# The last tile of a gated MLP: where its transposes stand in the queue, and in how many pieces its output is projected and stored

## The chip, the cores and the metric

The kernel runs on one core of a Trainium2 chip. A core has a matrix engine (PE in the profile; its weight loads are listed apart as PEld), VectorE (DVE), ScalarE (ACT), GpSimd (POOL) and SyncE (SP), each with its own queue of instructions that it works through in order. Engines wait for each other through semaphores. Transfers between the chip's DRAM and the on-chip memory are issued from a queue (here SP's or ScalarE's) and carried out by 16 DMA engines. [...]

The metric is the time of one execution on the device in microseconds, as the median over several runs; lower is better.

## The reference, cut to what matters

Two mixers follow each other on a sequence of 2048 rows with 640 columns, each behind a layer norm whose scale and shift come from a condition vector. The first is a long convolution by FFT; it ends before the part that the change touches. The second is a gated MLP with a mixing over the sequence:

```python
z = _gelu(jnp.einsum('bsd,df->bsf', x, w_in))
z1 = z[..., :Fh].copy()
z2 = _layernorm(z[..., Fh:], axis=-1)
g = jnp.einsum('ts,bsf->btf', w_sp, z2) + b_sp[None, :, None]
return jnp.einsum('bsf,fd->bsd', z1 * g, w_out)
```

with Fh = 864. The output is `x + gb * that`, in bf16. The change lies in the last two of these lines.

## The kernel before, in words

Everything up to `z1` and `z2` is ordered by a list written out by hand (`ORDER`) that a small planner walks through; the change does not touch it. When it is done, 16 tiles of `z1` and the normalised `z2` lie in on-chip memory, and so does `xt`, the residual.

The last stage, from about 195 us on, has no planner: its order is the order of the Python code. It goes over 16 tiles t of 128 rows of the output, and the functions `load_w`, `mix` and `project` each do a part for one tile.

`load_w(t)` fetches 128 rows of the mixing matrix by a transposing DMA on SP's queue, five tiles ahead.

`mix(t)` makes `g` for the tile in two halves of 432 columns (NFC = 2). Each half is 16 matmuls that accumulate over the sequence into one of four PSUM buffers (line 944). One VectorE instruction then adds the bias and multiplies with `z1`, and writes half of `u`, a bf16 tile of 128 x 896 (line 947; the last 32 columns are zeros from the start). Three buffers of `u` take turns. The next matmul needs `u` transposed. For tiles 0 to 14 a transposing DMA on SP's queue does it (line 950) and the function returns. For tile 15, `mix` has seven transposes on PE, 128 columns each, into a PSUM buffer `pt` (line 954), and a ScalarE copy from there to `uT` (line 955).

`project(t)` multiplies with the output weights, already scaled with `gb`. It has NH = 2 halves of HS = 320 columns. Each half is seven matmuls (line 962) into one of two PSUM buffers that take turns (tag `o`), and one VectorE addition of the residual into `ot` (line 964). One store of the 128 x 640 tile, 160 KB, follows on SP's queue (line 965).

The loop of lines 972 to 981 sets the order. In round t it emits `mix(t)`, then `load_w(t + 5)` while there is one, then `project(t - 2)`; two rounds more finish the projections. So behind the mixing of tile 15 PE's queue holds the seven transposes of tile 15 and then the projections of tiles 13, 14 and 15. A PSUM buffer is written again only when the instruction that read it has finished.

The end of the program (line 1007 in the profile) waits for all stores and then brings the engines together.

Of the kernel before, what the change touches and what calls it, by code (L numbers as in the profile page):

```python
# [10 lines left out]
ALU = mybir.AluOpType  # L11
# [112 lines left out]
def kernel(  # L124
# [20 lines left out]
    nc = tc.nc  # L145
    _, S, D = A_q.shape
# [3 lines left out]
    NT = S // P  # L150
    ND = D // P
    NFT = (Fh + P - 1) // P
    fsz = [min(P, Fh - i * P) for i in range(NFT)]
    SDIM = nc.vector.BN_STATS_DIM
    ADIM = nc.vector.BN_AGGR_DIM
    NH = 2
    HS = D // NH

    x_nat = A_q[0].rearrange("(n p) d -> p n d", p=P)
    out_nat = out[0].rearrange("(n p) d -> p n d", p=P)  # L160
# [12 lines left out]
    xt = persist.tile([P, NT, D], BF16)  # L173
# [31 lines left out]
    with ExitStack() as actx:  # L205
# [25 lines left out]
        op = plan.op  # L231
# [691 lines left out]
    UB = 3  # L923
# [5 lines left out]
    us = []  # L929
# [3 lines left out]
    wTs, uTs = {}, {}  # L933

    def load_w(t):
        wTs[t] = bwork.tile([P, NT, P], BF16, tag="wT", bufs=WB, name="wT")
        nc.sync.dma_start_transpose(wTs[t][:], B_w_sp[t * P:(t + 1) * P, :])

    def mix(t):
        u = us[t % UB]  # L940
        for fc in range(NFC):
            ps = psB.tile([P, 512], F32, tag="mm", bufs=4, name="ps")
            for s_ in range(NT):
                nc.tensor.matmul(ps[:, :FC], lhsT=wTs[t][:, s_, :], rhs=tl["z2_%d" % (s_ // TB)][:, s_ % TB, fc * FC:(fc + 1) * FC],  # L944
                                 start=(s_ == 0), stop=(s_ == NT - 1))
            sl = slice(fc * FC, (fc + 1) * FC)
            nc.vector.scalar_tensor_tensor(u[:, sl], ps[:, :FC], bcol[:, t:t + 1], z1[t][:, sl], op0=ALU.add, op1=ALU.mult)  # L947
        uTs[t] = bwork.tile([P, NFT, P], BF16, tag="uT", bufs=UB, name="uT")
        if t < NT - 1:
            nc.sync.dma_start_transpose(uTs[t][:], u[:])  # L950
            return
        pt = psB.tile([P, NFT, P], BF16, tag="pt", bufs=1, name="pt")
        for ft in range(NFT):
            nc.tensor.transpose(pt[:, ft, :], u[:, ft * P:(ft + 1) * P], ident[:])  # L954
        nc.scalar.copy(uTs[t][:], pt[:])  # L955

    def project(t):
        ot = bwork.tile([P, D], BF16, tag="ot", bufs=3, name="ot")
        for h in range(NH):
            ps = psB.tile([P, 512], F32, tag="o", bufs=2, name="po")  # L960
            for ft in range(NFT):
                nc.tensor.matmul(ps[:, :HS], lhsT=uTs[t][:fsz[ft], ft, :], rhs=w_o[:fsz[ft], ft, h * HS:(h + 1) * HS],  # L962
                                 start=(ft == 0), stop=(ft == NFT - 1))
            nc.vector.tensor_tensor(ot[:, h * HS:(h + 1) * HS], ps[:, :HS], xt[:, t, h * HS:(h + 1) * HS], op=ALU.add)  # L964
        nc.sync.dma_start(out_nat[:, t, :], ot[:])

    for t in range(WB - 1):
        load_w(t)
    w_o = wsp_pool.tile([P, NFT, D], BF16, name="w_o")
    for ft in range(NFT):  # L970
        nc.sync.dma_start(w_o[:fsz[ft], ft, :], B_w_out[ft * P:ft * P + fsz[ft], :])
    for t in range(NT + 2):
        if t < NT:
            mix(t)
        if t == 1:
            for ft in range(NFT):
                nc.vector.tensor_tensor(w_o[:fsz[ft], ft, :], w_o[:fsz[ft], ft, :], gb_bf[:fsz[ft], :], op=ALU.mult)
        if t + WB - 1 < NT:
            load_w(t + WB - 1)
        if t >= 2:  # L980
            project(t - 2)


# [28 lines left out]
```

## Time and profile before

| | |
|---|---|
| median of 6 runs | 326.12 us (325.81 to 326.99) |
| the profiled execution's own time | 326.19 us |
| its span, first to last instruction | 324.3 us |
| mean granted PE clock | 0.993 |
| PE busy, share of the span | 308.4 us, 95% |
| VectorE, ScalarE, GpSimd busy | 209.7, 148.2, 93.5 us |
| matmul of 128 x 432, line 944 | 346 ns, 512 of them |
| matmul of 128 x 320, line 962 | 299 ns, 224 of them |
| addition of 128 x 320, line 964 | 491 ns, 32 of them |
| store of 160 KB, from issue to landing | 1.8 to 3.0 us, median 2.2, 16 of them |

The durations of matmuls overlap, since they are pipelined: the time from the start of one to the start of the next is shorter than a row's duration. All times inside an execution are given in us from the start of the span. A wait is put down to the instruction whose semaphore came last.

### The profile page before, as it was taken

How to read it: one execution, taken by the hardware profiler on the slowest of the kernel's cores; microseconds unless marked ns; L12 is line 12 of the kernel's file. 1: busy time of each engine (PE TensorE's matmuls, PEld its weight loads, DVE VectorE, ACT ScalarE, POOL GpSimd, SP SyncE). 2: the span in 40 equal slices, each digit the busy share in tenths (PEclk: the TensorE clock that was granted, in tenths of full speed). 3: DMA queues.
4: the chain of work that ended last, by engine and by line, in shares of the span. 5: the costliest groups of instructions: out<-in, count | busy, mean ns of one | idle time of the engine just before them, and what ended most of it. 6: DMA issues, size and time to landing. Idle time of an engine off the chain costs nothing.

```text
span 324.3 us, 6365 instructions
## 1 busy us (share of the span) xinstructions
PE 308.4 (95%) x2574; PEld 205.5 (63%) x2582; DVE 209.7 (65%) x463; ACT 148.2 (46%) x255; POOL 93.5 (29%) x121
## 2 busy tenths in 40 slices
PE   5969999899999998899999999999999999999995
PEld 2556789778889896655555555555555555555553
DVE  8966999999999998899676773432222223333223
ACT  4756999897779755396578582000000000000010
POOL 2440725559799898310111120000000000000000
PEclk9989999999999999999999999999999999999999
DMA  6999997996687876004408970675654555522231
GB/s 114 207 258 264 258 276 196 241 249 172 116 232 151 260 143 226 4 3 79 82 1 147 197 202 2 122 142 107 155 115 115 113 115 114 113 51 49 49 51 61
DMA packets 128580, 44.99 MB, mean 139 GB/s; under 512 B 117704, under 2 KB 127784, under 8 KB 128552
## 3 DMA queue, kind: packets, MB, share of 16 engines
q1 hardware_dynamic: 125528, 41.78, 58.6%
q10 hardware_dynamic: 3024, 2.82, 2.6%
q8 instruction: 20, 0.33, 0.4%
q14 instruction: 8, 0.07, 0.1%
HBM read 16.11 MB, written 5.24 MB: 66 GB/s over the span
## 4 chain that ended last, share of the span: by engine, by line
PE 74%; DVE 12%; DMA 7%; SPq 4%; issue 1%; ACT 1%; POOL 0%; DVEq 0%; POOLq 0%
PE ps L944 29%; PE pu L240 15%; PE pz L240 13%; PE po L962 9%; DMA ZT<-Z 5%; PE sm L240 5%; SPq L511 3%; PE s L240 2%; DVE Tf L457 2%; DVE T L457 2%; DVE st L570 2%; DMA X<-in_A_ssm_k_dram 2%; DVE big L543 1%; DVE X L243 1%; PE sm L823 0%
## 5 line engine op out<-in xcount | busy, mean ns | idle before, releaser
L944 PE MATMUL ps<-X,wT 128*128 128x432 bf16 x512 | 95.7, 346 | 0.0
L944 PEld LDWEIGHTS <-wT 128*128 128x128 bf16 x512 | 50.1, 98 | 42.2
L955 ACT COPY uT<-pt 128x896 bf16<-128x896 bf16 x1 | 0.9, 906 | 118.0 <-PE pt L954 118.0
L240 PE MATMUL pu<-X,M 128*128 128x128 bf16 (+1 forms) x480 | 46.8, 239 | 1.5 <-DVE T L457 0.9
L240 PEld LDWEIGHTS <-Z 128*128 128x128 bf16 x320 | 31.1, 98 | 26.6 <-DVE Z L832 0.4
L240 PEld LDWEIGHTS <-M 128*128 128x128 bf16 x480 | 37.5, 99 | 7.0 <-issue 1.6
L947 DVE SCALAR_TENSOR_TENSOR u<-ps,bcol,G 128x432 bf16<-128x432 f32 x18 | 12.0, 668 | 42.2 <-PE ps L944 42.2
L243 ACT CAST X<-s 128x1024 bf16<-128x1024 f32 x32 | 32.7, 1021 | 4.4 <-PE s L240 4.3
L962 PE MATMUL po<-w_o,uT 128*128 128x320 bf16 (+1 forms) x224 | 32.8, 299 | 0.0
L240 PE MATMUL pu<-big,Z 128*128 128x432 bf16 x160 | 32.8, 346 | 0.0
L466 POOL TENSOR_TENSOR W<-Tf 128x256 bf16<-128x256 f32 x38 | 27.9, 754 | 16.5 <-DVE Tf L457 15.8
L240 PE MATMUL pz<-big,Z 128*128 128x432 bf16 x160 | 32.6, 346 | 0.0
L947 DVE SCALAR_TENSOR_TENSOR u<-ps,bcol,M 128x432 bf16<-128x432 f32 x14 | 9.3, 667 | 30.2 <-PE ps L944 30.2
L240 PEld LDWEIGHTS <-G 128*128 128x128 bf16 x360 | 26.9, 98 | 1.9
L962 PEld LDWEIGHTS <-uT 128*128 128x128 bf16 (+1 forms) x224 | 21.8, 98 | 9.8
L243 ACT CAST KH<-pu 128x512 bf16<-128x512 f32 x40 | 23.0, 595 | 6.4 <-PE pu L240 6.2
L457 DVE TENSOR_TENSOR Tf<-pu,KH 128x1024 f32<-128x1024 f32 x20 | 24.2, 1218 | 1.6 <-PE pu L240 1.1
L457 DVE TENSOR_TENSOR T<-pu,KH 128x1024 bf16<-128x1024 f32 x20 | 24.2, 1216 | 0.5 <-PE pu L240 0.5
L964 DVE TENSOR_TENSOR ot<-po,xt 128x320 bf16<-128x320 f32 x32 | 15.7, 491 | 13.5 <-PE po L962 13.5
L240 PEld LDWEIGHTS <-X 128*128 128x128 bf16 x288 | 18.3, 99 | 8.3 <-DVE X L396 4.8
L243 ACT CAST Z<-pz 128x512 bf16<-128x512 f32 x35 | 20.3, 590 | 6.8 <-PE pz L240 6.5
L888 DVE BATCH_NORM_STATS2 stz<-X 128x6 f32<-128x432 bf16 x32 | 18.2, 592 | 7.1 <-ACT X L882 7.1
(143 smaller groups left out, 412.3 us busy)
## 6 DMA issues: line engine op xcount, KB each, us to landing
wm<-in_w_mod_dram SPq DMA_DIRECT2D x4, 800.0 KB, 5.6
out_dram<-ot SPq DMA_DIRECT2D x16, 160.0 KB, 2.2
big<-in_B_w_in_dram SPq DMA_DIRECT2D x2, 1080.0 KB, 8.2
X<-in_A_ssm_k_dram SPq DMA_DIRECT2D x4, 512.0 KB, 6.3
kv_scr<-big SPq DMA_DIRECT2D x4, 512.0 KB, 3.1
X<-kv_scr SPq DMA_DIRECT2D x4, 512.0 KB, 4.6
xt<-in_A_q_dram SPq DMA_DIRECT2D x3, 640.0 KB, 6.7
wm<-in_w_mod_dram ACTq DMA_DIRECT2D x2, 800.0 KB, 7.4
```

Of the source, the lines that this page charges most:

```text
L240: nc.tensor.matmul(o, lhsT=w, rhs=x, start=start, stop=stop)
L243: (e.copy if e is nc.scalar else e.tensor_copy)(dst, src)
L457: e.tensor_tensor(T_[:], tl[pu][:, :, :, None, :].to_broadcast([P, KP, 2, 2, DU]), tl[KH][:, :, None, :, :].to_broadcast([P, KP, 2, 2, DU] ...
L466: e.tensor_tensor(tl[W][:, :, o, :], T_[:, :, 0, o, :], T_[:, :, 1, 1 - o, :], op=ALU.add if o else ALU.subtract)
L511: e.dma_start_transpose(tl[name][:, o + h * m:o + (h + 1) * m], src[0, h * m:(h + 1) * m, dt * P:(dt + 1) * P])
L543: e.tensor_tensor(vsl, tl[ps][:], vsl, op=ALU.mult)
L570: e.bn_stats(out=st[:, a, :], in_=xt[:, n, a * HS:(a + 1) * HS])
L888: op("D", "stz", lambda e, i=i, n=n, fc=fc: e.bn_stats(out=stz[:, n, fc, :], in_=tl[z2][:, i, fc * FC:(fc + 1) * FC]), r=[(z2, (i, fc))], ...
L944: nc.tensor.matmul(ps[:, :FC], lhsT=wTs[t][:, s_, :], rhs=tl["z2_%d" % (s_ // TB)][:, s_ % TB, fc * FC:(fc + 1) * FC], start=(s_ == 0), st ...
L947: nc.vector.scalar_tensor_tensor(u[:, sl], ps[:, :FC], bcol[:, t:t + 1], z1[t][:, sl], op0=ALU.add, op1=ALU.mult)
L962: nc.tensor.matmul(ps[:, :HS], lhsT=uTs[t][:fsz[ft], ft, :], rhs=w_o[:fsz[ft], ft, h * HS:(h + 1) * HS], start=(ft == 0), stop=(ft == NFT ...
L964: nc.vector.tensor_tensor(ot[:, h * HS:(h + 1) * HS], ps[:, :HS], xt[:, t, h * HS:(h + 1) * HS], op=ALU.add)
```

## The change

The transposes and the copy of tile 15 leave `mix` and become a function `turn_last`, which the loop calls in round 15 behind `project(13)`. In `project`, tile 15 has three pieces in place of two: 320, 160 and 160 columns, each with its own seven matmuls and its own addition. Each piece of tile 15 is stored by itself as soon as it is added: the first and the third from SP's queue, the second from ScalarE's. The other tiles are projected and stored as before, and the two PSUM buffers of tag `o` stay two.

```diff
         uTs[t] = bwork.tile([P, NFT, P], BF16, tag="uT", bufs=UB, name="uT")
         if t < NT - 1:
             nc.sync.dma_start_transpose(uTs[t][:], u[:])
-            return
+
+    def turn_last(t):
+        u = us[t % UB]
         pt = psB.tile([P, NFT, P], BF16, tag="pt", bufs=1, name="pt")
         for ft in range(NFT):
             nc.tensor.transpose(pt[:, ft, :], u[:, ft * P:(ft + 1) * P], ident[:])
...
     def project(t):
         ot = bwork.tile([P, D], BF16, tag="ot", bufs=3, name="ot")
-        for h in range(NH):
+        last = t == NT - 1
+        for i, (lo, hi) in enumerate(((0, HS), (HS, HS + HS // 2), (HS + HS // 2, D)) if last else ((0, HS), (HS, D))):
             ps = psB.tile([P, 512], F32, tag="o", bufs=2, name="po")
             for ft in range(NFT):
-                nc.tensor.matmul(ps[:, :HS], lhsT=uTs[t][:fsz[ft], ft, :], rhs=w_o[:fsz[ft], ft, h * HS:(h + 1) * HS],
+                nc.tensor.matmul(ps[:, :hi - lo], lhsT=uTs[t][:fsz[ft], ft, :], rhs=w_o[:fsz[ft], ft, lo:hi],
                                  start=(ft == 0), stop=(ft == NFT - 1))
-            nc.vector.tensor_tensor(ot[:, h * HS:(h + 1) * HS], ps[:, :HS], xt[:, t, h * HS:(h + 1) * HS], op=ALU.add)
-        nc.sync.dma_start(out_nat[:, t, :], ot[:])
+            nc.vector.tensor_tensor(ot[:, lo:hi], ps[:, :hi - lo], xt[:, t, lo:hi], op=ALU.add)
+            if last:
+                (nc.scalar if i == 1 else nc.sync).dma_start(out_nat[:, t, lo:hi], ot[:, lo:hi])
+        if not last:
+            nc.sync.dma_start(out_nat[:, t, :], ot[:])
...
         if t >= 2:
             project(t - 2)
+        if t == NT - 1:
+            turn_last(t)
```

## The prediction

> **What bounds the kernel now.** I read the whole-span table first: PE is busy 95% of the span, every other engine 65% or less. But the change touches only the last tile, so what counts is the chain of work that ended last, in order of time, for the last 20 us (start us, length us, what):
>
> ```profile
> 308.12 5.86 PE ps L944 x32
> 313.97 0.02 issue
> 314.00 0.68 DVE u L947
> 314.68 0.05 issue
> 314.72 0.40 PE pt L954 x4
> 315.12 5.74 PE po L962 x42
> 320.86 0.02 issue
> 320.88 0.49 DVE ot L964
> ```
>
> The mixing of tile 15 ends on PE, the chain leaves PE for 0.7 us of VectorE, returns to PE for four transposes and 42 projection matmuls (tiles 13, 14, 15; 14 each), and ends with one addition on VectorE. So PE is the bound here except in two places: the hop through VectorE, and everything behind 320.86. The timeline shows the hop (start, length, engine, line, operands; in brackets the idle time and its releaser):
>
> ```profile
> 313.61 0.34 PEld L954 LDWEIGHTS <-u 128*128 128x128 bf16 x3
> 313.79 0.33 PE L954 MATMUL pt<-ident,u 128*128 128x128 bf16 x3
> 314.00 0.67 DVE L947 SCALAR_TENSOR_TENSOR u<-ps,bcol,G 128x432 bf16<-128x432 f32 x1 [2.25 <-PE ps L944]
> 314.72 0.23 PEld L954 LDWEIGHTS <-u 128*128 128x128 bf16 x4 [0.77 <-DVE u L947]
> 314.72 0.40 PE L954 MATMUL pt<-ident,u 128*128 128x128 bf16 x4 [0.60 <-DVE u L947]
> 314.95 0.57 PE L962 MATMUL po<-w_o,uT 128*128 128x320 bf16 x3
> 315.15 0.91 ACT L955 COPY uT<-pt 128x896 bf16<-128x896 bf16 x1 [117.98 <-PE pt L954]
> ```
>
> Three transposes need only columns that the first multiply-add wrote; the fourth needs the second one, which ends at 314.67. PE waits, and tile 13's projection, whose operands are there since about 302 (the transpose by DMA was issued at 299.19 and such a one lands after 2.9), stands behind it in PE's queue. ScalarE does nothing here but the copy.
>
> The third view is the end: VectorE's last two additions and SP's last issue in the timeline, then SP's waits at the program's end (count, min/median/max ns, first and last start), then the DMA share and rate over 321.3 to 324.3 us in 40 slices of 0.075 us.
>
> ```profile
> 319.93 0.49 DVE L964 TENSOR_TENSOR ot<-po,xt 128x320 bf16<-128x320 f32 x1 [0.46 <-PE po L962]
> 320.88 0.49 DVE L964 TENSOR_TENSOR ot<-po,xt 128x320 bf16<-128x320 f32 x1 [0.46 <-PE po L962]
> ```
> ```profile
> 321.40 0.33 SPq L965 DMA_DIRECT2D out_dram<-ot  x1
> ```
> ```profile
> L1007 SPq EVENT_SEMAPHORE  x7: 17/28/1435, 321.8 to 324.2; - x7
> ```
> ```profile
> DMA  0000000000003999995100000000000000000000
> GB/s 0 0 0 0 0 0 0 0 0 0 0 0 119 341 341 375 375 375 205 52 0 0 0 0 0 0 0 0 0 0 0 0 0 0 0 0 0 0 0 0
> ```
>
> The last store (160 KB, 128 rows of 1280 B) is issued at 321.40; its data move from about 322.2 to 322.75; SP is released near 323.24 (321.8 + 1.435), 1.8 us after the issue; then 1.06 us of closing to 324.3. So 0.8 us pass ahead of the data, 0.5 us are data, 0.45 us follow.
>
> **Part 1: tile 13's projection moves ahead of the transposes.** PE's queue becomes mixing 15, projection 13, seven transposes, projection 14, projection 15. Spacing of 320-column matmuls: 5.74/42 = 0.137 us, so 14 take 1.91. Transposes without a wait: four weight loads in 0.23 us, so 0.057 each, seven 0.40. Today from the first transpose to the first projection matmul: 314.95 - 313.79 = 1.16. Gain: 1.16 - 0.40 = 0.76 us.
>
> Its cover: projection 13 now stands over the 0.93 us until the multiply-add's end with 1.91. Without it the 0.76 is back. The moved step is seven transposes and one ScalarE copy; it issues no DMA and nothing is queued behind it on ScalarE but the new store. Projection 13 brings forward two additions and one store on SP by 1.16 us: the first addition would start near 314.95, just behind the multiply-add that ends at 314.67, and SP's queue has been empty since 309. What is late next: the transposed tile 15 is needed at projection 15, and only projection 14 is left to hide the copy. New times: projection 13 from 313.79, transposes from 315.70, projection 14 from 316.10 to 318.02; the last transpose ends near 316.27, the copy (0.91) near 317.21; the weights of projection 15 load from about 317.9. Slack 0.65 us, cost nothing.
>
> **Part 2: three pieces for tile 15.** Piece 0 is unchanged (7 x 0.137 = 0.96; starts 318.02, last matmul starts 318.84 and with its row's 0.30 ends 319.14; addition 319.16 to 319.65). Pieces 1 and 2 have 160 columns, a shape that the trace lacks. Between 128 columns (0.057 spacing, 219 ns long) and 320 (0.137, 299 ns) lies 0.070 spacing and 232 ns; seven take 0.49. Bounds: 0.057, as the transposes, and 0.098, one weight load's whole row; I take 0.070, since the transposes ran at 0.057 with the same weight loads. The addition of 160: the row for 320 is 491 ns, that for 512 from PSUM (multiply with v) 679, slope 0.98 ns a column, so 0.33 us (bounds 0.25, half of 491, and 0.49).
>
> The change adds one wait. There are two PSUM buffers for the pieces, so piece 2 needs the one of piece 0, free when its addition is done: 319.65, plus the 0.05 that the chain shows from VectorE to PE: 319.69. Unhindered it would start at 318.97 + 0.49 = 319.46. The stall is 0.23 us; nothing but piece 2 stands behind it on PE. Its last matmul starts 320.11, ends 320.34; addition 320.37 to 320.70. Today that end is 321.37; so of the 0.76, 0.67 arrive here: splitting costs 0.09 on the compute side (0.23 stall, less 0.16 shorter addition, rest rounding and matmul ends).
>
> **Part 3: the stores.** One of 160 KB becomes 80 KB (SP, rows of 640 B, issued about 319.68), 40 KB (ScalarE's queue, 320 B, about 320.03) and 40 KB (SP, 320 B, about 320.73). An issue takes 0.33 us on SP and 0.345 on ScalarE (row of kv_scr), both idle by then; data start 0.8 us after an issue, so the three data phases do not overlap (320.5, 320.8, 321.5). Only the last one sets the end. Today each of 16 DMA engines has 8 rows of 1280 B at 375/16 = 23.4 B/ns: 55 ns a row, 0.44 us. For 320 B rows the nearest row is the load of kv_scr, 256 B rows: at its plateau of 285 GB/s, 14.4 ns each, over its whole 2.4 us and 128 rows an engine 19 ns. Eight make 0.12 to 0.15 us. Gain 0.3 us (between 0.42, and a loss bounded below).
>
> [...]
>
> **Sum.** 0.76 - 0.09 + 0.30 = 0.97 us. The span goes from 324.3 to 323.3 and the profiled execution's 326.19 (1.9 around the span, unchanged) to 325.22. That execution stands 0.07 over the median of 326.12, so the median becomes 325.15, 0.30% lower. About 0.2% (0.65 us) is what a measurement of this kernel can tell from no change.
>
> **Rivals.**
> A. The sum above: 325.15; own range 324.8 to 325.4. Chance 0.62.
> B. The store is all latency: a 40 KB store also lands 1.8 us after its issue. For: 1.25 of its 1.8 us are not data, and stores of one size range from 1.8 to 3.0. Against: the data phase is plainly 0.5 us. Gain 0.67, 325.45, on the edge of what can be told. Chance 0.20.
> C. The other side: the 320 B rows of the last store are written slowly, row after row. [...] Against: packets of 256 B flow at 14 to 19 ns on the read side. Chance 0.08.
> D. Part 1 acts, but piece 2 waits for piece 1's addition too, if the buffer's release is counted to VectorE's newest instruction: start 320.04, end of the last addition 321.05, gain 0.32 + 0.30 = 0.62, 325.5. Against: today projection 14 starts at 316.87 while tile 13's second addition, begun at 317.06, is still to come, so releases are counted singly. Chance 0.10.
>
> **How the numbers follow.** Repeated runs before spread from 325.81 to 326.99, so a median may be off by 0.2 to 0.3. A falls below -0.2% nine times in ten (0.56), B and D half the time (0.10 and 0.05), C never: faster 0.71. Within 0.2%: what is left of A, B and D, 0.06 + 0.10 + 0.05 = 0.21. Slower: C, 0.08. Range: below, the full 0.76, a free split and 0.42 of store, 1.2, with a drift of 0.3, is 324.6; above, B or D with a drift is 325.85; C is left out.
>
> **What would show it.** Part 1: no idle PE before the transposes, 42 projection matmuls and seven transposes without a gap, the copy's end ahead of projection 15. Part 2: idle PE of about 0.2 us before piece 2, released by the first addition; the last addition near 0.33 us, ending 0.67 earlier against the span's start. Part 3: SP's long wait at the end down from 1.435 to 1.1, and ScalarE's store not the last to land; it would be only if it took over 2.1 us. The prediction is wrong if that wait grows, if PE still idles ahead of the transposes, or if the stages ahead of 308 us shift by more than 0.3 us.

## The result, and the profile after

The changed kernel takes 325.87 us (median of 35 runs) where the kernel before took 326.43 (72 runs): the ratio is 0.9977, with a 95% interval from 0.9966 to 0.9987, so 0.42 to 1.1 us of gain. The ratio is taken over the fast runs (one of the changed kernel, at 329.11 us, was slow), so it is not the quotient of the two medians. The forecast, 325.15 for 326.12 or 0.9970, lies inside the interval.

The profiled execution has a span of 322.8 us instead of 324.3. That is 1.5 us, but not all of it is the change's doing. The chain of waits of the changed kernel, in order of time (start us, length us, what):

```profile
307.65 5.84 PE ps L944 x32
313.50 1.91 PE po L965 x14
315.40 0.39 PE pt L956 x7
315.80 2.88 PE po L965 x21
318.68 0.02 issue
318.70 0.50 DVE ot L967
319.20 0.04 issue
319.24 0.66 PE po L965 x7
319.90 0.02 issue
319.93 0.33 DVE ot L967
```

The hop through VectorE's multiply-add has left the chain, and PE goes from the mixing into projection 13 (line numbers behind 950 have moved: 965 is the projection, 967 its addition, 956 the transposes, 957 the copy, 969 the stores in pieces). A new hop has come in near the end: the addition of 318.70, then the third piece's matmuls at 319.24. The timeline of the same stretch:

```profile
313.33 2.07 PE L965 MATMUL po<-w_o,uT 128*128 128x320 bf16 x14
313.54 0.67 DVE L947 SCALAR_TENSOR_TENSOR u<-ps,bcol,G 128x432 bf16<-128x432 f32 x1 [2.25 <-PE ps L944]
315.24 0.55 PE L956 MATMUL pt<-ident,u 128*128 128x128 bf16 x7
315.83 0.91 ACT L957 COPY uT<-pt 128x896 bf16<-128x896 bf16 x1 [119.12 <-PE pt L956]
318.70 0.81 DVE L967 TENSOR_TENSOR ot<-po,xt 128x320 bf16<-128x320 f32 x2 [0.46 <-PE po L965]
319.24 0.44 PEld L965 LDWEIGHTS <-uT 128*128 128x128 bf16 x6 [0.23 <-issue]
319.54 0.36 ACTq L969 DMA_DIRECT2D out_dram<-ot  x1
319.93 0.33 DVE L967 TENSOR_TENSOR ot<-po,xt 128x160 bf16<-128x160 f32 x1 [0.42 <-PE po L965]
```

The transposes run as one group without idle time; the copy ends at 316.74, well ahead of projection 15, which follows the 14 matmuls of projection 14 near 317.5. Ahead of the third piece's weight loads stand 0.23 us of idle time. The row calls it "issue", that is, it names no releaser; the chain does, as it goes back from the matmuls to the addition.

To keep the last tile apart from all that lies before, two stretches are compared. C runs from the start of tile 15's second multiply-add to the end of the last addition, T from there to the end of the span. A span of 324.3 us is rounded to a tenth, too coarse for T; a stretch that is left open at its end shows where the span ends to a hundredth (before, then after; stretch, length, busy time and number of instructions of the five engines, granted clock, DMA share, GB/s):

```profile
319.00:324.28 5.28, 1.85 (x14) 1.08 (x12) 1.45 (x3) 0.00 (x0) 0.00 (x0) 0.87 0.18 62
```
```profile
319.00:322.82 3.82, 0.80 (x10) 0.46 (x7) 0.84 (x3) 0.00 (x0) 0.00 (x0) 0.87 0.28 86
```

Before: C = 320.88 + 0.49 - 314.00 = 7.37 and T = 324.28 - 321.37 = 2.91. After: C = 319.93 + 0.33 - 313.54 = 6.72 and T = 322.82 - 320.26 = 2.56. So 0.65 + 0.35 = 1.00 us come from the change. The other 0.46 us (314.00 against 313.54) had been gained before the multiply-add even began. C and T are sums of rounded rows and good to about 0.02 us; the expectations of the runs below were written with T from the rounded spans, 2.93 before and 2.54 after.

The tail, in SP's waits of the changed kernel from 300 us on (us in total, times, longest):

```profile
SPq L1015 <- DMA out_dram<-ot: 1.1, 2, 0.6
SPq L1015 <- PEq L1015: 0.6, 2, 0.4
```

Before, the first of these was 1.5 in one piece. There are two pieces now, as SP waits for ScalarE's store first. The last store lands 1.5 us after its issue instead of 1.8. Its data, in the DMA view from 320.2 to 322.6 us in slices of 0.06 us, for an issue at 320.29:

```profile
GB/s 352 214 96 43 144 251 193 70 5 0 0 0 0 0 0 107 208 240 107 22 0 0 0 0 0 0 0 0 0 0 0 0 0 0 0 0 0 0 0 0
```

The first group is the 80 KB store's end and ScalarE's store; the second group is the last store, from about 321.1, 0.8 us after the issue, to 321.4. How long one DMA engine is busy with the last store is told by the queue's share in a stretch that holds this store alone: 3.0 us from 321.3 before, 0.45 us from 321.0 after (packets, MB, share of 16 engines):

```profile
q1 hardware_dynamic: 144, 0.16, 15.6%
```
```profile
q1 hardware_dynamic: 144, 0.04, 37.1%
```

That is 0.47 us an engine before and 0.17 after, for eight rows and one small packet each.

### The profile page after: what moved, and what is told of

Same layout as the page of the kernel before. It is cut to its first block, busy times and chain, and to the rows that moved or that the text cites. A ratio compares the mean times of both kernels' runs of the same rounds, so it can differ in the third digit from the quotient of the medians.

```text
span 322.8 us, 6384 instructions
## 1 busy us (share of the span) xinstructions
PE 307.8 (95%) x2581; PEld 205.8 (64%) x2589; DVE 209.8 (65%) x464; ACT 148.2 (46%) x255; POOL 93.6 (29%) x121
## 4 chain that ended last, share of the span: by engine, by line
PE 74%; DVE 10%; DMA 7%; SPq 4%; ACT 2%; issue 1%; POOL 0%; DVEq 0%; POOLq 0%; ACTq 0%
PE ps L944 29%; PE pu L240 15%; PE pz L240 13%; PE po L965 9%; DMA ZT<-Z 5%; PE sm L240 5%; SPq L511 3%; PE s L240 2%; DVE T L457 2%; DVE Tf L457 2%; DMA X<-in_A_ssm_k_dram 2%; DVE st L570 1%; DVE big L543 1%; DVE X L243 1%; ACT X L243 1%
## 5 line engine op out<-in xcount | busy, mean ns | idle before, releaser
L965 PE MATMUL po<-w_o,uT 128*128 128x320 bf16 (+2 forms) x231 | 33.2, 295 | 0.1
L967 DVE TENSOR_TENSOR ot<-po,xt 128x320 bf16<-128x320 f32 (+1 forms) x33 | 15.9, 482 | 12.7 <-PE po L965 12.7
```

The source lines that it names most:

```text
L965: nc.tensor.matmul(ps[:, :hi - lo], lhsT=uTs[t][:fsz[ft], ft, :], rhs=w_o[:fsz[ft], ft, lo:hi], start=(ft == 0), stop=(ft == NFT - 1))
L967: nc.vector.tensor_tensor(ot[:, lo:hi], ps[:, :hi - lo], xt[:, t, lo:hi], op=ALU.add)
```

## The experiments

In all of them the code up to tile 15's mixing is the same. C and T are taken from each trace as above, one execution of each kernel. Four pairs of kernels have the same matmuls, copy and additions over all of C, and agree in it to 0.01 us: 6.72 and 6.71, 6.61 twice, 6.47 twice and 6.49 twice.

**The order alone.**

```diff
     def project(t):
         ot = bwork.tile([P, D], BF16, tag="ot", bufs=3, name="ot")
-        last = t == NT - 1
+        last = False
```

> The transposes stand behind projection 13, tile 15 is projected and stored as before. Two stretches are read: C, from the start of tile 15's second multiply-add to the end of the last addition (before 7.37 us, after 6.72), and T, from there to the end of the span (before 2.93, after 2.54). Theory (terms add up): C = 7.37 - 0.76 = 6.61, T = 2.93, so 0.76 us less than before, ratio near 0.9977. Rival 1 (the gain is the smaller last store; the wait only moves to the copy ahead of projection 15): C near 7.3, ratio within 0.1% of 1. Rival 2 (the changed kernel's 1.5 us shorter span is the change's doing, also ahead of the last tile): the multiply-add of tile 15 starts near 313.5 again, not near 314.0.

Measured: ratio 0.9979, interval 0.9962 to 0.9997. The chain ends so:

```profile
315.54 1.91 PE po L965 x14
317.44 0.39 PE pt L956 x7
317.84 3.83 PE po L965 x28
321.67 0.02 issue
321.69 0.49 DVE ot L967
```

The multiply-add starts at 315.57, the last addition ends at 322.18, the span ends at 325.11: C = 6.61, T = 2.93. The order brings 0.76 us in C, which is what was worked out, and nothing in T. Rival 1 falls, and so does rival 2: this kernel's span is longer than that of the kernel before although its last tile is shorter by 0.74, since its multiply-add came 1.6 us later. What moves the multiply-add is not the change (see the last section).

**The pieces alone.** The transposes go back to where they stood.

```diff
         if t < NT - 1:
             nc.sync.dma_start_transpose(uTs[t][:], u[:])
+        else:
+            turn_last(t)
...
             project(t - 2)
-        if t == NT - 1:
-            turn_last(t)
```

> Three pieces and three stores for tile 15, but the transposes stay ahead of projection 13. Theory (terms add up): C = 7.37 + 0.04 to 0.09 (a stall of 0.23 us ahead of the third piece, a shorter last addition), T = 2.54, so 0.30 to 0.35 us less than before, ratio near 0.9990. Rival 1 (the smaller store is the main gain): 0.9977 or less. Rival 3 (splitting costs as much as the smaller store saves): ratio 1.000, T near 2.9.

Measured: ratio 0.9991, interval 0.9975 to 1.0007. From the trace (multiply-add at 315.14, last addition from 322.30 to 322.63, end of the span 325.18): C = 7.49, T = 2.55, a net 0.24 us less than before, where 0.30 to 0.35 were expected. The interval alone couldn't tell this from no change; the trace shows both terms: splitting costs 0.12 in C, over the 0.04 to 0.09 expected, and the smaller last store saves 0.36 in T. Rival 3 had T near 2.9 and falls; rival 1 asked for three times the trace's sum. The two parts add up: 0.74 for the order and 0.24 for the pieces are 0.98 of the 1.00 of the whole change. That the pieces gain anything rests on the traces; in the timed runs the order alone (0.9979) and the whole change (0.9977) can't be told apart.

**Three pieces, one store.**

```diff
-            if last:
-                (nc.scalar if i == 1 else nc.sync).dma_start(out_nat[:, t, lo:hi], ot[:, lo:hi])
-        if not last:
-            nc.sync.dma_start(out_nat[:, t, :], ot[:])
+        nc.sync.dma_start(out_nat[:, t, :], ot[:])
```

> The changed kernel, three pieces, but one store of 160 KB behind the third addition. Theory (the last store's bytes set T): C = 6.72 as in the changed kernel, T = 2.93 as before. Rival (T is shorter for another reason, as the order of the queues at the end): T = 2.54.

Measured, one execution: multiply-add at 313.75, last addition from 320.14 to 320.46, end of the span 323.38; C = 6.71, T = 2.92. T is back at the value of before, so it follows the last store and not the pieces or their order. Pieces without stores of their own only cost: 0.10 in C against the order alone.

**Two pieces, two stores.**

```diff
-        for i, (lo, hi) in enumerate(((0, HS), (HS, HS + HS // 2), (HS + HS // 2, D)) if last else ((0, HS), (HS, D))):
+        for i, (lo, hi) in enumerate(((0, HS), (HS, D)) if last else ((0, HS), (HS, D))):
```

> Transposes behind projection 13, tile 15 in two pieces of 320 columns, each stored at once: the first by SP, the second (80 KB, rows of 640 B) from ScalarE's queue. Theory (the store's data phase shrinks with its bytes): C = 6.61, T between 2.54 and 2.93, near 2.7. Rival (what shortens T is the third piece's short rows or that SP's queue was drained earlier): T = 2.9. Rival (ScalarE's queue lands later): T above 2.93.

Measured: ratio 0.9970, interval 0.9957 to 0.9983; C = 6.61 (314.11 to 320.72), T = 2.76 (end of the span 323.48), the store of 80 KB landing 1.6 us after its issue. T lies between, as the bytes do. Its sum of 9.37 us is 0.09 over that of the three pieces (9.28); the timed runs, whose intervals overlap widely, cannot rank the two.

**The cover of the copy taken away.** The transposes stand behind projection 14.

```diff
-        if t == NT - 1:
-            turn_last(t)
+        if t == NT:
+            turn_last(t - 1)
```

> The changed kernel with the transposes of tile 15 behind projection 14, so that nothing hides the ScalarE copy. Theory (projection 14 is the cover of the copy): PE idle of about 1.1 us ahead of projection 15, released by the copy, C = 6.72 + 1.1 = 7.8, T = 2.54. Rival (the copy is hidden or overlaps piece by piece): C below 7.0.

Measured, one execution. The timeline:

```profile
318.14 0.56 PE L956 MATMUL pt<-ident,u 128*128 128x128 bf16 x7
318.73 0.91 ACT L957 COPY uT<-pt 128x896 bf16<-128x896 bf16 x1 [121.03 <-DMA out_dram<-ot]
319.69 2.35 PE L965 MATMUL po<-w_o,uT 128*128 128x320 bf16 x21 [1.00 <-ACT uT L957]
```

PE is idle for 1.00 us, released by the copy; C = 7.90 (314.52 to 322.42), T = 2.56 (end of the span 324.98), and the last tile takes 10.46, more than the 10.28 of before. (The bracket at the copy names a store that landed at the same moment. The copy needs nothing of it, and starts 0.03 us behind the end of the transposes, as it does in the changed kernel, 0.04.) So the place between projections 13 and 14 is the only one of the three tried that hides both the multiply-add and the copy.

**A third PSUM buffer.** PSUM is where the matmuls' results stand until the addition reads them (`ot<-po` in the rows above).

```diff
-            ps = psB.tile([P, 512], F32, tag="o", bufs=2, name="po")
+            ps = psB.tile([P, 512], F32, tag="o", bufs=3, name="po")
```

> The changed kernel with three PSUM buffers for the projection's pieces in place of two. Theory (the third piece waits for the first one's addition through its buffer): idle PE ahead of the third piece gone, C = 6.72 - 0.22 = 6.50, T = 2.54. Rival (VectorE's additions in a row set the end, the buffer doesn't): C stays at 6.7, since the second piece's addition cannot start sooner.

Measured: ratio 0.9963, interval 0.9949 to 0.9978. The end of the chain:

```profile
315.39 0.39 PE pt L956 x7
315.78 3.85 PE po L965 x35
319.63 0.03 issue
319.66 0.33 DVE ot L967
```

All 35 matmuls follow each other; C = 6.47 (313.52 to 319.99), T = 2.56 (end of the span 322.55). The wait of 0.23 us was the buffer's: C falls by 0.25. It also gives the spacing of the 160-column matmuls: the 21 of 320 columns take 2.88 in the changed kernel's chain, so the 14 narrow ones take 0.97, 0.069 us each.

**A thin last piece.** Pieces of 320, 256 and 64 columns, with three buffers.

```diff
-        for i, (lo, hi) in enumerate(((0, HS), (HS, HS + HS // 2), (HS + HS // 2, D)) if last else ((0, HS), (HS, D))):
-            ps = psB.tile([P, 512], F32, tag="o", bufs=2, name="po")
+        for i, (lo, hi) in enumerate(((0, HS), (HS, 576), (576, D)) if last else ((0, HS), (HS, D))):
+            ps = psB.tile([P, 512], F32, tag="o", bufs=3, name="po")
```

> The changed kernel with three PSUM buffers and pieces of 320, 256 and 64 columns, so that the last store has 16 KB in rows of 128 B. Theory (data phase by bytes and rows that flow at 14 to 19 ns): the last addition waits for the one of 256 columns, C = 6.5 + 0.13 = 6.63, T = 2.45. [...]

Measured, one execution: C = 6.49 (315.40 to 321.89), T = 2.77 (end of the span 324.66). T is above the 2.45 of the theory, and a store of 16 KB, the smallest tried, lands later than one of 40: 1.7 us after its issue, where the changed kernel's last one took 1.5. The rows of 128 B might be slow to write by themselves; this run does not show whether they are. But the issues also show the middle store next to it: ScalarE's 64 KB were issued at 321.79, SP's 16 KB at 321.91, 0.12 us later, so that the two may be in each other's way. One more run separates the two reasons.

**The thin piece without its neighbour.** The middle piece's store is left out.

```diff
-            if last:
-                (nc.scalar if i == 1 else nc.sync).dma_start(out_nat[:, t, lo:hi], ot[:, lo:hi])
+            if last and i != 1:
+                nc.sync.dma_start(out_nat[:, t, lo:hi], ot[:, lo:hi])
```

> Pieces of 320, 256 and 64 columns with three PSUM buffers as in the run with a thin last piece, but the middle piece is not stored at all (its output is left out). Theory (the thin last store was late because the middle one, issued 0.12 us earlier, was moving its data): T = 2.45 and a landing 1.4 us after the issue. Rival (rows of 128 B are slow to write by themselves): T stays at 2.8, the landing at 1.7.

Measured, one execution: C = 6.49 (315.60 to 322.09), T = 2.56 (end of the span 324.65). The DMA issues from 317 us on, this kernel's and then those of the thin piece with its neighbour (KB each, us to landing):

```profile
out_dram<-ot SPq DMA_DIRECT2D x1, 80.0 KB, 1.6
out_dram<-ot SPq DMA_DIRECT2D x1, 16.0 KB, 1.4
```
```profile
out_dram<-ot SPq DMA_DIRECT2D x1, 80.0 KB, 1.6
out_dram<-ot ACTq DMA_DIRECT2D x1, 64.0 KB, 1.7
out_dram<-ot SPq DMA_DIRECT2D x1, 16.0 KB, 1.7
```

T is 0.21 under the run with the middle store, so the lateness was the neighbour's. What of the neighbour it was, its data or what follows them, this run doesn't tell. The 128 B rows alone land after 1.4 us, the soonest of all stores here: at eight rows an engine these short rows show no delay of their own. But T misses the expected 2.45 by 0.11: it is no shorter than with 40 KB, 2.56 in the changed kernel, so a last store smaller than 40 KB gained nothing.

**All stores from SP**, with three buffers.

```diff
-                (nc.scalar if i == 1 else nc.sync).dma_start(out_nat[:, t, lo:hi], ot[:, lo:hi])
+                nc.sync.dma_start(out_nat[:, t, lo:hi], ot[:, lo:hi])
```

> Three PSUM buffers and three pieces, all three stores from SP's queue. Theory (SP has 0.16 us to spare between two issues of 0.33): C = 6.47, T = 2.6 as with ScalarE's queue. Rival (the second queue is what lets the last store start at once): T larger by 0.1 to 0.3.

Measured, one execution: C = 6.47 (314.94 to 321.41), T = 2.70 (end of the span 324.11), 0.14 over the T of the same kernel with ScalarE's queue. SP's three issues run from 320.62 for 1.28 us. The second and the third take 0.38 us each and not 0.33; so the last begins at 321.52, 0.11 us behind the addition's end at 321.41, where it is 0.02 with ScalarE's queue (320.01 behind 319.99). The later start, 0.09, and the longer issue, 0.05, make up the 0.14. SP had no time to spare and the theory was wrong; the rival's 0.1 to 0.3 holds. T of like stores issued from both queues lies between 2.52 and 2.56 in five traces, so 2.70 stands out though it is one execution.

**The transposing DMA for tile 15 as well**, with three pieces and three buffers.

```diff
         uTs[t] = bwork.tile([P, NFT, P], BF16, tag="uT", bufs=UB, name="uT")
-        if t < NT - 1:
-            nc.sync.dma_start_transpose(uTs[t][:], u[:])
+        nc.sync.dma_start_transpose(uTs[t][:], u[:])
...
-        if t == NT - 1:
-            turn_last(t)
```

> The kernel with three PSUM buffers and three pieces, but tile 15 is turned by the transposing DMA like all other tiles, so that the seven transposes and the ScalarE copy are gone. Theory (PE is the bound from the last multiply-add on, and the DMA has the 3.8 us of projections 13 and 14 to land): issued 0.69 us after the multiply-add's start, landed 2.9 us later, that is 3.6 us after it, projection 15 due 3.63 us after it; C = 6.47 - 0.39 = 6.1 with a wait of 0.1 at most, T = 2.57, ratio near 0.995. Rival (the transposing DMA lands later, up to the 4.3 us that one of them took, or collides with the store of tile 13): PE idles ahead of projection 15, C at 6.5 or more, no gain over three buffers alone.

Measured: ratio 0.9923, interval 0.9893 to 0.9952. The chain from the mixing on, and the DMA's issue in the timeline:

```profile
315.01 5.77 PE po L964 x49
320.78 0.02 issue
320.80 0.32 DVE ot L966
```
```profile
315.05 0.67 DVE L947 SCALAR_TENSOR_TENSOR u<-ps,bcol,G 128x432 bf16<-128x432 f32 x1 [2.25 <-PE ps L944]
315.74 1.22 SPq L949 DMA_TRANSPOSE uT<-u  x1
318.66 1.90 PEld L964 LDWEIGHTS <-uT 128*128 128x128 bf16 x21 [0.17 <-DMA uT<-u]
```

All 49 matmuls of the three projections run through in 5.77 us: 35 at 0.137 and 14 at 0.069 make 5.76, so no matmul waits. But the transposed tile came only just in time: the weight loads of projection 15 stood idle for 0.17 us until it had landed, 2.9 us after its issue. One that took the 4.3 us of the slowest in the kernel before would have held PE up by more than 1 us (an estimate, 4.3 - 2.9). C = 6.07 (315.05 to 321.12), T = 2.52 (end of the span 323.64), together 8.59 against 10.28 before and 9.28 after the change; the kernel with three buffers has 9.03. The interval lies below that of the changed kernel and overlaps that of three buffers at its edge. It comes from six runs, and its middle asks for more (2.5 us) than the trace gives (1.69, a ratio of 0.9948, inside the interval).

## Why the prediction was right, step by step

| step | worked out | measured (traces) |
|---|---|---|
| the wait for the multiply-add leaves PE's path | -0.76 | -0.76 (C, order alone) |
| stall ahead of piece 2 | 0.23 | 0.23 (idle row), 0.25 (third buffer) |
| spacing of 160-column matmuls | 0.070 | 0.069 |
| addition of 160 columns | 0.33 | 0.33 |
| splitting, on the compute side | +0.09 | +0.11 (6.72 - 6.61), +0.12 (pieces alone) |
| last store | -0.30 | -0.30 (data), -0.35 (T), -0.36 (pieces alone) |
| sum | -0.97 | -1.00 in the trace; -0.42 to -1.1 in the timed runs |

Part 1 and its cover. The copy ended at 316.74 and was due near 317.5, a slack of 0.7 to 0.8 us against the 0.65 worked out; behind projection 14 it costs 1.00 us of idle PE.

Part 2. The third piece waits for the first one's addition, and only for that: with the second addition counted too (rival D) the matmuls could not have begun at 319.24, when that addition was still running (318.70 to 319.51 for both).

Part 3. The data phase of the last store was to shrink from 0.44 us an engine to 0.12 to 0.15, and shrank from 0.47 to 0.17: both ends lie a little higher, the difference of 0.30 is as forecast. A row of 320 B took about 21 ns, more than the 14 to 19 of the 256 B loads that it was taken from. T fell by 0.35, so some 0.05 fell away elsewhere; where, the runs do not tell. T against the last store's bytes is 2.91 to 2.93 us for 160 KB, 2.76 for 80, 2.52 to 2.56 for 40 (2.70 with all stores from SP), 2.56 for 16 when undisturbed. The loss that the forecast also allowed for showed in no run: with a smaller last store T was 2.52 to 2.77, always under the 2.91 of before. ScalarE's store landed 1.6 us after its issue, short of the 2.1 from which it would have set the end. Rival B (the store is all latency) asked for an unchanged T throughout and falls.

Rival C was the one on the other side, with rows of 320 B that are written slowly; from the thin piece alone (T 2.77) it looked right, and the run without the middle store (2.56) showed another cause. To eat the 0.67 us that parts 1 and 2 bring, a row would have had to take 139 ns (an estimate: the 0.44 us of the data phase before and the 0.67, over eight rows); it took about 21.

The timed gain, 0.75 us at the middle of its interval, is less than the trace's 1.00, but 1.00 lies inside the interval. So do the 0.67 of rival B and the 0.62 of rival D: the timed runs alone could not have picked the sum above from these, the traces did. The four variants that were timed beside the same runs of the kernel before were shorter in their last tile by 0.74, 0.24, 1.25 and 0.91 us (order, pieces, three buffers, two pieces) and were timed at 0.9979, 0.9991, 0.9963 and 0.9970, which by the sums should be 0.9977, 0.9993, 0.9962 and 0.9972. So the sums carry over to the timed runs; a single ratio here is worth no more than its interval.

One of the prediction's own signs of being wrong did appear: the stages ahead of 308 us stand 0.47 us earlier (the mixing of tile 15 starts at 307.65, before at 308.12), more than the 0.3 that it allowed. The code there is the same in both kernels, and the last section shows that such shifts come and go between executions. So the sign was badly chosen, and the span of the profiled execution, which was forecast at 323.3 us and came out at 322.8, owes half a microsecond to chance.

## What to carry to other kernels

An in-order queue that waits for one hop through another engine can do ready work first (0.76 us here): look for the place where the moved step has cover on both sides, and work out both, since one place further cost all of the gain and more (10.46 us for the last tile against 10.28 before). When the last output is cut into pieces, as here, give every piece its own PSUM buffer (0.25 us in C), let two queues share the issues (0.14 in T), and keep the last store small (40 KB was enough here, 16 KB gave the same T of 2.56) and clear of a neighbour issued just before it (0.21 in T, with 0.12 us between the issues). And if a last tile is treated apart from the others, work out whether the special path is needed at all: here the ordinary transposing DMA, which landed 2.9 us after its issue, fitted behind the two projections, without any slack, and the last tile became 0.44 us shorter (9.03 to 8.59, both with three buffers). Without the transposes PE's queue goes from the mixing into projections 13 and 14 by itself, so part 1's gain lay open to the kernel before in this way too; that kernel with nothing but the transposing DMA was not run.

## What the runs showed of the hardware that was not expected

Tile 15's multiply-add started anywhere from 313.52 to 315.60 us over the twelve traces, though the code ahead of it is one and the same. A good part of this goes with the granted PE clock. Stages of the order-alone kernel and of the changed one (columns as in the stretches above):

```profile
129.06:132.47 3.41, 3.10 (x102) 2.82 (x99) 3.23 (x13) 0.01 (x1) 1.66 (x3) 1.00 0.02 5
132.47:139.30 6.83, 6.26 (x54) 3.39 (x53) 4.66 (x14) 3.19 (x6) 0.95 (x3) 0.50 0.01 2
```
```profile
129.06:132.47 3.41, 3.10 (x101) 2.84 (x100) 3.23 (x13) 0.13 (x1) 1.65 (x3) 1.00 0.03 5
132.47:139.30 6.83, 6.05 (x66) 3.53 (x64) 5.86 (x19) 4.63 (x8) 1.07 (x3) 1.00 0.01 2
```

In nine of the twelve traces the clock fell to 0.50 at a place between 130.7 and 133.6 us, for 3.41 us, and in the order-alone kernel for twice that, 6.83. Where it did not (the kernel before, the changed one, the one with three buffers), it fell early in the span instead: to 0.50 from 22.5 us in the kernel before and from 21.5 in the changed one, while in the third the mean over 20 to 25 us was 0.66; two kernels had both. From the last instruction of line 457, near 121 us, to the first matmul of line 944, near 195, pass 73.8 to 74.0 us in the three traces without the later drop and 75.0 to 76.1 in the nine with it, the most in the order-alone kernel. The rest of the scatter is there before 122 us.

PE was not idle ahead of the drop: in the 3.41 us before it, in the order-alone kernel, PE's rows are busy for 3.10. Nearly all of these matmuls, 97 of 102, have only 16 columns; but the changed kernel has 96 of them among its 101 in the same stretch and kept its clock at 1.00. What sets the drop off the runs do not show. For the reader of a profile it means that a difference of two spans is not yet the effect of a change of one microsecond: it has to be read from a mark just ahead of the change.
